# A windowed attention and a Fourier mixing on one core: the attention's pace by a table of units, one input's searches over more projections, weight splits a projection earlier

## The chip, the cores and the metric

The kernel runs on one core of a Trainium2 chip. The metric is the device time of one execution in microseconds, and a kernel's time is the median of its runs. The engines are TensorE (PE; PEld is its weight load), VectorE (DVE), ScalarE (ACT), GpSimd (POOL) and SyncE (SP), which here issues most of the DMAs.

## What is computed

Two independent results stand side by side in the output. The first is attention over 2048 rows with 32 heads of 32 elements, in which each row sees the 256 rows up to itself. The second is the real part of a two-dimensional Fourier transform, written as products with given matrices.

```python
qkv = (x @ wqkv).reshape(B, S, 3, H, Dh)            # S 2048, D 1024, H 32, Dh 32
scores = einsum("bhqd,bhkd->bhqk", q, k) * Dh ** -0.5
mask = (i - j >= 0) & (i - j < 256)
p = softmax(where(mask, scores, -1e9))
a = (einsum("bhqk,bhkd->bhqd", p, v)) @ wo

u = einsum("bsd,ed->bse", xb, dft_hid_re)
w = einsum("bsd,ed->bse", xb, dft_hid_im)
b = einsum("ts,bse->bte", dft_seq_re, u) - einsum("ts,bse->bte", dft_seq_im, w)
out = concatenate([a, b], axis=-1)
```

Inputs and outputs are float32. The first input and its weights are drawn eight times larger than usual.

## The kernel before

**Numbers.** Every operand of a large product is split into two float16 parts: ACT writes the scaled high part and DVE the rest (`split`). A product is then three matmuls (`PASSES`). A split needs a scale, and the scale needs the operand's largest magnitude: DVE searches each piece (`top`), a transpose on PE spreads the result (`scale_of`; its tile is called `pt_...`), and DVE makes the scale.

**Projections.** The list `order` holds 96 of them, n = 0 to 95: q, k and v for eight groups of four heads. Each is 24 matmuls of 512 columns into one of three PSUM banks; ACT and DVE empty the bank (`yq`, `yk`, `yv`) and SP stores it to DRAM (`qk`, `vs`). What else must happen meanwhile is entered in `tasks` with `at(n, ...)`, and is issued ahead of projection n. A weight that projection n uses first is loaded at n - 6 (`w_load`), searched at n - 4 (`w_top`), and scaled and split at n - 2 (`w_finish`). `scan("B", 16, 22, 1)` loads the 16 pieces of the second input at n = 22 to 37 and searches each one projection later; its scale follows at n = 40. From n = 41 on (`xp`) that scale is used to split the same input.

**Units.** The Fourier part follows as four rounds of twelve units, (p, c) = (0,0), (0,1), (1,0), (1,1). In a round, x0 to x3 are the hidden transform of four pairs of row blocks and c0 to c7 the sequence transform of eight pairs. A unit is seven products of twelve matmuls (`seven`), 84 in all. The work for unit n + 1 is done during unit n: for a c unit DVE and ACT search and split the two loaded pieces (`u_top`, `u_step`); for an x unit SP only loads finished pieces (`x_left`, tiles `un_a`, `un_c`, `un_b` and a part of `reg`). So DVE has little of this kind to do in c7 and x0. In x3 and c0 it also turns the x units' results into operands (`t_last`, line 795). In round (0,0) the c units store their results plainly through SP; later rounds add them to what stands in DRAM by accumulating stores that POOL issues (`store`, line 1069). The eight units `po` of the output projection end the program.

**Attention.** It is a generator, `attention()`, of 256 blocks: a block is one tile of 128 rows for two heads. A block goes through these steps: PE writes scores (`s`, `far`; three buffers), DVE masks (L237) and finds the row maximum (L239), ACT makes the bias (L242) and the exponentials (L249), ACT and DVE split them into `hl` (L252, L253; three buffers), SP transposes `hl` into `t` by DMA (L255), POOL masks two corners (`z_step`, L267 and L269), and PE multiplies with v (`pv`) six blocks later (`LAG`). Every fourth block, `o_step` divides by the row sum, splits, transposes through SP (`ot`) and stores (`ots`).

**Pace.** `tick(n)` is called after every few matmuls of projections and units. It adds `n * rate[0]` to a counter and advances the generator by half a block for each whole number. So the generator's instructions stand between those of the projections and units, and PE, which works in program order, waits there if a block's input is late. Before, `rate[0]` is `base * 0.6` in projections and `base` in units, with 0.2 of it in x3. By the formula `base` is 0.1217, so a projection takes 24 x 0.1217 x 0.6 / 2 = 0.88 blocks and a unit 84 x 0.1217 / 2 = 5.1, x3 1.0. A block may start only when its k and v are stored (`ready`).

The order of instructions on DVE, ACT, POOL and SP is laid down by a scheduler when the program is built; the programmer's order is its starting point.

Of the kernel before, what the change touches and what calls it, by code (L numbers as in the profile page):

```python
# [25 lines left out]
NG = H // HG  # L26
# [3 lines left out]
NCH = S // CH  # L30
QB = CH // P
# [7 lines left out]
LAG = 6  # L39
# [14 lines left out]
def fused_kernel(ctx: ExitStack, tc: tile.TileContext, xa, wqk, wv, wo, xb, wd, cs, out):  # L54
# [44 lines left out]
    def bank(name):  # L99
        nbank[0] += 1  # L100
        return ps_m.tile([P, CH], F32, tag=f"m{nbank[0] % 3}", name=name)
# [260 lines left out]
    def product(ps, lhs, rhs, n=ND):  # L362

        m = 0
        for d in range(n):
            for hl, hr in PASSES:
# [6 lines left out]
    order = ([("q", g, c) for c in range(NCH) for g in range(4)] + [("k", 0, c) for c in range(NCH)]  # L373
             + [("v", 0, t) for t in range(NT)]
             + [("k", g, c) for g in (1, 2, 3) for c in range(NCH)]
             + [("v", 1, t) for t in range(NT)]
             + [(kd, g, c) for g in range(4, NG) for kd in "qk" for c in range(NCH)])
    tasks = {}

    def at(n, f, *args):  # L380
        tasks.setdefault(n, []).append((f, args))


    START = 24
    LAST = 4
    SHARE = {"p": 0.6, "x": (1.0, 1.0, 1.0, 0.2), "c": 1.0}
    base = 2.0 * (NG * NCH * 2 * QB + 2 * LAG) / (
        24 * (len(order) - START) * SHARE["p"] + 84 * (4 * sum(SHARE["x"]) + (24 + LAST - 0.7) * SHARE["c"]))
    rate = [base * SHARE["p"]]

    wraw, wun, vw, xraw, held = {}, {}, {}, {}, {}
    scw = const.tile([P, 2, NG, 2], F32, name="scw")
# [128 lines left out]
        use.setdefault((kd, g), n)  # L521
    for (kd, g), n in use.items():
        if kd in "qk" and n >= 4:
            at(n - 6, w_load, kd, g)
            at(n - 4, w_top, kd, g)
            at(n - 2, w_finish, kd, g)
    for g in range(NG):
        at(max(use["q", g], use["k", g], 11), scores_scale, g)

# [20 lines left out]
    at(20, wv_known)  # L550
    def scan(key, k, n, step):
        for i in range(k):
            at(n + step * i, scan_load, key, i)
            at(n + step * i + 1, scan_top, key, i, k)
        at(n + step * (k - 1) + 3, scan_scale, key)

    scan("wd1", 8, 9, 1)
    scan("B", 16, 22, 1)
    scan("wd0", 8, 40, 4)
    scan("wo", 8, 73, 2)  # L560
    at(72, fa_known)
# [278 lines left out]
    with tc.tile_pool(name="pa", bufs=2) as pa:  # L840
        def qk_out(kd, g, c, ps, f):
            y = pa.tile([P, 2, CH], F16, tag="yq", name=f"y{kd}{g}_{c}")
            behind_act[:] = [nc.scalar.activation(y[:, 0], ps, AF.Copy, scale=f)]
            behind[:] = [vec(nc.vector.scalar_tensor_tensor, y[:, 1], ps, f, y[:, 0],
                             op0=ALU.mult, op1=ALU.subtract)]
            a = "qk".index(kd)
            for j, part in enumerate(((0, 1, 0), (0, 0, 1))[a]):
                nc.sync.dma_start(qk[g, c, j, :, :, a].rearrange("d h t -> (d h) t"), y[:, part])

        def d_out(g):  # L850
            qk_out("q", g, 0, direct.pop(g), f0[:, g:g + 1])

        w_top("q", 0)
        x_top(0, (0, 1, 2, 3))
        d_mm(0, range(0, 4))
        w_scale("q", 0)
        d_mm(0, range(4, 8))
        w_top("q", 1)
        d_mm(1, range(0, 1))
        x_scale(0)  # L860
        d_known(0)
        d_mm(1, range(1, 3))
        w_scale("q", 1)
        d_known(1)
        d_out(0)
        w_split("q", 0)
        w_top("q", 2)
        d_mm(1, range(3, 8))
        x_top(1, (0, 1))
        d_out(1)  # L870
        d_mm(2, range(0, 2))
        w_scale("q", 2)
        d_known(2)
        x_top(1, (2, 3))
        d_mm(2, range(2, 8))
        w_top("q", 3)
        d_mm(3, range(0, 2))
        x_scale(1)
        x_split(1, (0, 1))
        d_out(2)  # L880
        d_mm(3, range(2, 4))
        w_scale("q", 3)
        d_known(3)
        x_split(1, (2,))
        d_mm(3, range(4, 8))
        x_split(1, (3,))
        w_split("q", 1)
        d_out(3)

        for n, (kd, g, c) in enumerate(order):  # L890
            if n < 4:
                continue
            if n == 22:
                first_cm.__exit__(None, None, None)
                wx_pool = ctx.enter_context(tc.tile_pool(name="wx", bufs=1, side="right"))
                cellx["wx"] = wx_pool.tile([P, 3 * 2 * 4 * CH], F16, name="wx")
                att_cm = tc.tile_pool(name="att", bufs=2, side="right")
                cell["att"] = att_cm.__enter__()
                agen[0] = attention()
                upcoming[0] = next(agen[0])  # L900
            for f, args in tasks.pop(n, ()):
                f(*args)
            ps = bank(f"p{kd}{g}_{c}")
            if kd == "v":
                t = c
                product(ps, lambda h, d: xin[:, t // 4, h, d, t % 4 * P:t % 4 * P + P],
                        lambda h, d: reg2[:, g, h, d])
                y = pa.tile([P, H // 2, VW], F16, tag="yv", name=f"yv{g}_{t}")
                nc.gpsimd.memset(y[:, :, DH:DH + 1], 1.0)
                nc.gpsimd.memset(y[:, :, 2 * DH + 1:], 0.0)  # L910
                f = vf[:, g, t // 4:t // 4 + 1]
                pv = ps.rearrange("p (h d) -> p h d", d=DH)
                behind_act[:] = [nc.scalar.activation(y[:, :, :DH], pv, AF.Copy, scale=f)]
                behind[:] = [nc.vector.scalar_tensor_tensor(y[:, :, DH + 1:2 * DH + 1], pv, f, y[:, :, :DH],
                                                            op0=ALU.mult, op1=ALU.subtract)]
                nc.sync.dma_start(vs[t, :, g * (H // 2) * VW:(g + 1) * (H // 2) * VW],
                                  y.rearrange("p h w -> p (h w)"))
            else:
                u = wun[kd, g]
                product(ps, lambda h, d: u[:, h, d], lambda h, d: xin[:, c, h, d])  # L920
                qk_out(kd, g, c, ps, DOWN if kd == "q" else kf[:, c:c + 1])
            if kd == "v" and g == 0 and c % 4 == 3:
                ready.add((0, c // 4))
            if kd == "v" and g == 1 and c == NT - 1:
                pass
            if kd == "k" and g > 0:
                ready.add((g, c))
# [101 lines left out]
    with tc.tile_pool(name="pb", bufs=1) as pb:  # L1029
# [15 lines left out]
        for r in range(4):  # L1045
            x0, c0 = 12 * r, 12 * r + 4
            for j in range(4):
                n = x0 + j
# [5 lines left out]
            for j in range(8):  # L1054
                n = c0 + j
# [18 lines left out]

        x_left(0, "t")
        for n, (kind, p, c, i) in enumerate(units):
            rate[0] = base * (SHARE["x"][i] if kind == "x" else SHARE["c"])
            if kind == "x":
                y1, y2 = ytile(), ytile()

                def x_hook(pos):
                    (t_last if i > 1 else t_now)(i, pos, y2, y1)
                    hook(n, pos)

                if i < 2:
                    for turn in range(4):
                        do(n + 1, turn, t_then, i, turn, y2, y1)
                seven(f"p1_{n}", i, uns.pop(n), slot, y1, y2, 4.0 * DOWN, lambda t, y: None, x_hook)
                continue
            if p == 1 and c == 1:  # L1090
                if i == LAST:

                    while agen[0] is not None:
                        if next(agen[0], 0) == 0:
                            agen[0] = None
                    att_cm.__exit__(None, None, None)
                    late.append(ctx.enter_context(tc.tile_pool(name="late", bufs=8, side="right")))
                    raw = [[load_raw(wo[b % 2, 2 * (b // 2) + k], [2, CH], f"wo{b}_{k}", late[0]) for b in range(4)]
                           for k in range(2)]
                    for k in range(2):  # L1100
                        for j, f in enumerate(wo_blocks(raw[k], k)):
                            turn = 2 + (7 * k + j) * 3 // 2
                            do(n + turn // 7, turn % 7, f)
                    do(n + 2, 3, o_load, 0)
                    do(n + 2, 5, o_load, 1)
                    do(n + 3, 2, o_blocks, late, 0)
            y1, y2 = ytile(), ytile()
            f = fu.pop(n)

            def out_y(t, y):  # L1110
                dst, src = out[t * P:t * P + P, D:], y.rearrange("p e c -> p (e c)")
                if p == 0 and c == 0:
                    nc.sync.dma_start(dst, src)
                else:
                    do(n + 1, t % 2 == 0, store, dst, src)

            seven(f"p2_{n}", i, uns.pop(n), lambda pos: tsum[:, TPOS[pos]], y1, y2, f, out_y,
                  lambda turn: hook(n, turn))
# [61 lines left out]
```

## Time and profile before

| | us |
|---|---|
| median of three runs (1760.23 to 1774.22) | 1770.59 |
| the profiled execution | 1775.21 |
| its span | 1773.5 |
| DVE busy | 1381.1 (78%) |
| ACT busy | 1116.0 (63%) |
| POOL busy | 431.5 (24%) |

The first projection of the list that the loop runs starts about 35 us into the span, the units at 561.1 us and `po` at 1623.5 us. The shares above are means over stages that differ, so the prediction reads windows: a window row gives a stretch of time, its length, each engine's busy time in it with the number of instructions, the clock that TensorE was granted (1.00 is full), the mean busy share of the DMA engines and GB/s. A busy PE is modelled, since matmuls are pipelined. In a timeline row stand the start, the duration, the engine and line, and in brackets how long the engine sat idle before and what released it; SPq is the time that SP's queue takes to issue a DMA, not the transfer.

### The profile page before, as it was taken

The numbers are of one execution on the slowest core, as the hardware profiler recorded it, in microseconds if no ns is written. First come the engines' busy times: TensorE is split into PE (matmuls) and PEld (weight loads), VectorE is DVE, ScalarE is ACT, GpSimd is POOL, SyncE is SP. The second block draws the span as 40 slices with busy tenths as digits, with TensorE's granted clock in tenths as the row PEclk, the third lists the DMA queues.
The fourth block names the chain that finished last, engine by engine and source line by source line (L and its number), as shares of the span: only waits on it lengthen the run. The fifth ranks groups of instructions, "written<-read, shape, count | busy, mean of one in ns | idle before, by whom it ended". The sixth has DMA issues, their size and how long they took to land.

```text
span 1773.5 us, 30898 instructions
## 1 busy us (share of the span) xinstructions
PE 1710.9 (96%) x10980; PEld 854.1 (48%) x10980; DVE 1381.1 (78%) x2365; ACT 1116.0 (63%) x1939; POOL 431.5 (24%) x698
## 2 busy tenths in 40 slices
PE   9999999999999999999999989999898998999998
PEld 4444454545545545555544544545444444444443
DVE  7878987888894899985998866899686697586542
ACT  3335565665564888886878866888685686463322
POOL 0000221322132223332333423325243323100000
PEclk9999999999999999999999999999999999999999
DMA  9649999999999849999999999959989966854431
GB/s 344 199 158 281 323 283 300 286 270 310 270 253 259 198 100 210 213 209 237 194 282 172 207 163 229 206 115 186 186 171 204 205 144 105 231 99 95 131 95 72
DMA packets 473084, 363.32 MB, mean 205 GB/s; under 512 B 377440, under 2 KB 410208, under 8 KB 471648
## 3 DMA queue, kind: packets, MB, share of 16 engines
q1 hardware_dynamic: 466016, 336.17, 76.2%
q0 software_dynamic: 6912, 25.17, 8.9%
q8 instruction: 86, 1.41, 0.3%
q14 instruction: 70, 0.57, 0.1%
HBM read 178.52 MB, written 109.31 MB: 162 GB/s over the span
## 4 chain that ended last, share of the span: by engine, by line
PE 59%; DVE 18%; DMA 12%; ACT 5%; issue 4%; SPq 1%; POOL 1%; DVEq 0%; ACTq 0%; POOLq 0%
PE p_a L113 15%; PE pv L113 9%; PE p_b L113 7%; DMA t<-hl 7%; PE pq L113 7%; PE pk L113 6%; PE po_a L113 5%; PE p_c L113 4%; PE po_b L113 2%; PE s L113 2%; DVE hl L253 2%; DVE mx L239 2%; DVE reg L795 2%; DVE raw_u L752 1%; DVE y L996 1%
## 5 line engine op out<-in xcount | busy, mean ns | idle before, releaser
L249 ACT ACTIVATE s<-s,bias,escs 128x256 f32<-128x256 f32 (+1 forms) x512 | 270.1, 528 | 11.7
L253 DVE TENSOR_TENSOR hl<-s,hl 128x512 f16<-128x512 f32 (+1 forms) x256 | 170.6, 667 | 92.6 <-ACT hl L252 91.8
L113 PE MATMUL p_a<-reg,un_c 128*128 128x512 f16 x960 | 229.5, 381 | 7.7 <-ACT y L994 7.6
L267 POOL TENSOR_SCALAR_AFFINE_SELECT z<-t 128x512 f16<-128x512 f16 x224 | 171.9, 770 | 248.6 <-PE pv L113 128.2
L242 ACT ACTIVATE bias<-mx,pshift,escs 128x2 f32<-128x2 f32 x256 | 98.3, 384 | 168.2 <-DVE mx L239 165.7
L113 PEld LDWEIGHTS <-reg 128*128 128x128 f16 x1344 | 129.4, 98 | 143.0 <-issue 3.0
L246 POOL TENSOR_SCALAR mark<-bias 128x1 f32<-128x1 f32 x128 | 50.9, 398 | 570.3 <-ACT bias L242 547.3
L252 ACT ACTIVATE hl<-s 128x512 f16<-128x512 f32 (+1 forms) x256 | 148.8, 581 | 55.2 <-DMA t<-hl 49.8
L269 POOL TENSOR_SCALAR_AFFINE_SELECT t<-t 128x512 f16<-128x512 f16 x224 | 174.3, 783 | 12.4
L113 PE MATMUL pk<-reg,wu_k 128*128 128x512 f16 x768 | 174.6, 381 | 2.7 <-DVE wu_k L120 2.7
L113 PEld LDWEIGHTS <-un_b 128*128 128x128 f16 x1152 | 110.0, 98 | 132.7 <-issue 12.6
L239 DVE TENSOR_REDUCE mx<-s 128x2 f32<-128x512 f32 (+1 forms) x256 | 171.0, 668 | 2.9
L113 PE MATMUL pv<-reg,reg 128*128 128x512 f16 x768 | 171.9, 379 | 0.0
L113 PEld LDWEIGHTS <-un_c 128*128 128x128 f16 x1152 | 110.0, 98 | 127.3 <-issue 12.3
L113 PEld LDWEIGHTS <-un_a 128*128 128x128 f16 x1152 | 110.2, 98 | 121.5 <-issue 7.1
L113 PE MATMUL pq<-reg,wu_q 128*128 128x512 f16 x672 | 150.0, 379 | 3.8 <-DVE yq L120 2.9
L113 PE MATMUL p_b<-reg,un_b 128*128 128x512 f16 x576 | 139.7, 382 | 11.9 <-DVE reg L795 4.9
L113 PE MATMUL p_a<-reg,un_a 128*128 128x512 f16 x576 | 138.4, 382 | 3.4 <-DVE y L996 3.4
L113 PE MATMUL p_c<-reg,un_a 128*128 128x512 f16 x576 | 136.5, 379 | 0.0
L113 PEld LDWEIGHTS <-qk 96*128 96x128 f16 x1056 | 88.3, 98 | 79.8 <-issue 10.6
L237 DVE COPY_PREDICATED s<-upper,far 128x256 f32<-128x256 uint32 x224 | 94.4, 421 | 35.7 <-PE s L113 35.4
L113 PEld LDWEIGHTS <-wu_k 128*128 128x128 f16 x768 | 74.5, 98 | 85.4 <-DVE wu_k L120 3.2
(196 smaller groups left out, 3076.4 us busy)
## 6 DMA issues: line engine op xcount, KB each, us to landing
raw_u<-in_cs_dram SPq DMA_DIRECT2D x64, 512.0 KB, 4.9
qk<-qk SPq DMA_DIRECT2D x64, 384.0 KB, 5.3
out_dram<-y POOLq DMA_DIRECT2D x36, 512.0 KB, 8.0
qk<-yq SPq DMA_DIRECT2D x96, 128.0 KB, 4.2
qk<-yk SPq DMA_DIRECT2D x96, 128.0 KB, 3.7
xs<-wx SPq DMA_DIRECT2D x24, 512.0 KB, 5.0
wds<-wx SPq DMA_DIRECT2D x20, 512.0 KB, 5.7
vs<-yv SPq DMA_DIRECT2D x32, 264.0 KB, 4.4
```

The source lines that it names most:

```text
L113: fixed[:] = [nc.tensor.matmul(*args, **kwargs)]
L237: nc.vector.copy_predicated(s[:, :, P:], upper2, d["far"] if nb == 3 else never2)
L239: nc.vector.tensor_reduce(mx, sv, axis=AX.X, op=ALU.max, negate=True)
L242: nc.scalar.activation(bias, mx, AF.Identity, bias=pshift, scale=es)
L246: marks[:] = [nc.gpsimd.tensor_scalar(mark, bias[:, 0:1], 1.0, None, op0=ALU.mult)]
L249: nc.scalar.activation(sv[:, h], sv[:, h], AF.Exp, bias=bias[:, h:h + 1], scale=es)
L252: nc.scalar.activation(hi, sv, AF.Copy)
L253: behind[:] = [nc.vector.tensor_tensor(lo, sv, hi, op=ALU.subtract)]
L267: nc.gpsimd.affine_select(out=z, in_=pk, compare_op=ALU.is_gt, fill=0.0, base=0, pattern=[[0, 4], [-1, P]], channel_multiplier=1)
L269: nc.gpsimd.affine_select(out=pk, in_=pk, compare_op=ALU.is_ge, fill=0.0, base=0, pattern=[[0, 4], [1, P]], channel_multiplier=-1)
L752: nc.vector.tensor_tensor(o, a, b, op=op)
L795: nc.vector.tensor_tensor(lo, src, hi, op=ALU.subtract)
```

## The change

```diff
     START = 24
     LAST = 4
-    SHARE = {"p": 0.6, "x": (1.0, 1.0, 1.0, 0.2), "c": 1.0}
-    base = 2.0 * (NG * NCH * 2 * QB + 2 * LAG) / (
-        24 * (len(order) - START) * SHARE["p"] + 84 * (4 * sum(SHARE["x"]) + (24 + LAST - 0.7) * SHARE["c"]))
-    rate = [base * SHARE["p"]]
+    FIRST = (7.5, 5.2, 4.8, 0.4)
+    SECOND = (1.8, 4.4, 4.4, 4.4, 4.4, 4.4, 4.4, 7.5)
+    EARLY = {n: (0.85, 1.1, 1.05, 0.9, 1.0, 1.1)[(n - START) // 12] for n in range(START, len(order))}
+    in_units = 4 * sum(FIRST) + 3 * sum(SECOND) + sum(SECOND[:LAST]) - 0.7 * SECOND[LAST - 1]
+    early = (NG * NCH * 2 * QB + LAG - in_units) / sum(EARLY.values())
+    rate = [0.0]
...
-            at(n - 6, w_load, kd, g)
-            at(n - 4, w_top, kd, g)
-            at(n - 2, w_finish, kd, g)
+            at(n - 7, w_load, kd, g)
+            at(n - 5, w_top, kd, g)
+            at(n - 3, w_finish, kd, g)
...
     def scan(key, k, n, step):
         for i in range(k):
-            at(n + step * i, scan_load, key, i)
-            at(n + step * i + 1, scan_top, key, i, k)
-        at(n + step * (k - 1) + 3, scan_scale, key)
+            at(n + int(step * i), scan_load, key, i)
+            at(n + int(step * i) + 1, scan_top, key, i, k)
+        at(n + int(step * (k - 1)) + 3, scan_scale, key)
...
-    scan("B", 16, 22, 1)
+    scan("B", 16, 17, 1.4)
...
+            rate[0] = 2 * early * EARLY.get(n, 0.85) / 24
             ps = bank(f"p{kd}{g}_{c}")
...
-            rate[0] = base * (SHARE["x"][i] if kind == "x" else SHARE["c"])
+            rate[0] = 2 * (FIRST if kind == "x" else SECOND)[i] / 84
```

`FIRST` and `SECOND` give the blocks of each x and c unit directly: 7.5 in x0 and in c7, 0.4 in x3, 1.8 in c0, 4.4 in c1 to c6. `in_units` comes to 190.6 blocks, so `early` is (262 - 190.6) / 72 = 0.99, and `EARLY` scales it for six stretches of twelve projections: 0.84, 1.09, 1.04, 0.89, 0.99, 1.09 blocks a projection. In the built program the score matmuls of 72 blocks now stand in projections, against 64; x0 and c7 hold 7 or 8, against 5 or 6; c0 holds 2, against 4 to 6; c1 to c6 of the first three rounds hold 26, 26 and 27, against 30, 30 and 31. In round (1,1) the last block's scores move from c0 to c1. The number of instructions of each kind stays as it was.

The searches of the second input now start five projections earlier, 16 of them over 22 projections, and end one projection later, at n = 39; the scale falls at n = 41, the projection in which it is first used. All steps of a q or k weight move one projection ahead.

**DVE, ahead of the second group of k weights.** The rows run from the emptying of one v projection's bank (`yv`) to the split of the first weight of group 1 (`wu_k`), which projection 36 uses; `yv_14` is the bank of projection 34. Before:

```order
L914 SCALAR_TENSOR_TENSOR yv_14_1815<-pv_14_1773,vf,yv_14_1815 128x16x32
L120 RECIPROCAL scw<-scw 128x1
L120 TENSOR_REDUCE top_B<-raw_B_1767 128x1
L477 TENSOR_SCALAR e_1_1913<-scw,sc_X 128x1
L239 TENSOR_REDUCE mx_1804<-s_1798 128x2
L120 SCALAR_TENSOR_TENSOR wx<-wx,vwd 128x1024
L253 TENSOR_TENSOR hl_1744<-s_1730,hl_1744 128x512
L301 TENSOR_REDUCE o_0_1_1846<-pv_1845 128x132
L120 SCALAR_TENSOR_TENSOR wu_k_1761<-raw_wk_1461,scw,wu_k_1761 128x1024
```

After the change the same stretch, from `yv_13` on, reads:

```order
L917 SCALAR_TENSOR_TENSOR yv_13_1744<-pv_13_1679,vf,yv_13_1744 128x16x32
L120 TENSOR_REDUCE top_B<-raw_B_1673 128x1
L120 SCALAR_TENSOR_TENSOR wx<-wx,vwd 128x1024
L237 COPY_PREDICATED s_1764<-upper,far 128x2x128
L120 SCALAR_TENSOR_TENSOR wu_k_1667<-raw_wk_1411,scw,wu_k_1667 128x1024
L316 TENSOR_TENSOR ohl_0_0_1725<-o_0_0_1540,ohl_0_0_1725 128x256
L754 TENSOR_TENSOR wx<-wx 128x1024
L239 TENSOR_REDUCE mx_1770<-s_1764 128x2
L917 SCALAR_TENSOR_TENSOR yv_14_1799<-pv_14_1755,vf,yv_14_1799 128x16x32
```

The split has moved from eight rows behind `yv_14` to four ahead of it.

**SP, in c7 of round (0,0).** The rows run from the first to the second piece of the next x0's operand (`un_a`, `un_c`). `t` is a block's transpose, `ot` and `ots` the transpose and store of four finished blocks, `vt` and `qk` a load of v and of q and k. Before:

```order
L747 DMA un_a<-xs 128x2048
L255 DMA_TRANSPOSE t_9343<-hl_9340 128x8x128
L1113 DMA out_dram<-y_6136 128x1024
L255 DMA_TRANSPOSE t_9417<-hl_9414 128x8x128
L211 DMA vt_1_2_9544<-vs 128x4x132
L205 DMA qk_1_2_9542<-qk 96x2048
L255 DMA_TRANSPOSE t_9458<-hl_9455 128x8x128
L318 DMA_TRANSPOSE ot_0_3_9504<-ohl_0_3_9501 128x4x128
L337 DMA ots<-ot_0_3_9504 128x512
L255 DMA_TRANSPOSE t_9531<-hl_9528 128x8x128
L747 DMA un_c<-xs 128x2048
```

After:

```order
L749 DMA un_a<-xs 128x2048
L337 DMA ots<-ot_0_3_9445 128x512
L255 DMA_TRANSPOSE t_9480<-hl_9477 128x8x128
L255 DMA_TRANSPOSE t_9528<-hl_9525 128x8x128
L255 DMA_TRANSPOSE t_9576<-hl_9573 128x8x128
L205 DMA qk_1_3_9691<-qk 96x2048
L255 DMA_TRANSPOSE t_9612<-hl_9609 128x8x128
L318 DMA_TRANSPOSE ot_1_0_9655<-ohl_1_0_9652 128x4x128
L749 DMA un_c<-xs 128x2048
```

In both programs `ots` stands one to four rows behind the `ot` that it waits for, and transposes of later blocks stand behind it. In this stretch three block transposes now follow each other with nothing between them.

## The prediction, made before the changed kernel ran

> **What bounds the kernel now.** The page first, then the windows cut at each unit's first matmul, then the waits. Two lines of the page, busy time by engine and the chain that ended last:
>
> ```profile
> PE 1710.9 (96%) x10980; PEld 854.1 (48%) x10980; DVE 1381.1 (78%) x2365; ACT 1116.0 (63%) x1939; POOL 431.5 (24%) x698
> PE 59%; DVE 18%; DMA 12%; ACT 5%; issue 4%; SPq 1%; POOL 1%; DVEq 0%; ACTq 0%; POOLq 0%
> ```
>
> PE leads, but only 59% of the chain is PE; the rest is what PE waits for. The matmuls are the same after the change and their number too, so only waits can come or go. The windows show where they are:
>
> ```profile
> core 0: us, PE busy (x) PEld busy (x) DVE busy (x) ACT busy (x) POOL busy (x), PEclk, DMA share, GB/s
> 208.20:217.90 9.70, 7.01 (x27) 2.68 (x25) 9.04 (x12) 3.52 (x6) 0.24 (x2) 0.82 0.95 247
> 518.00:526.40 8.40, 5.88 (x32) 2.91 (x31) 8.30 (x21) 6.19 (x11) 2.69 (x3) 1.00 1.03 302
> 644.60:668.20 23.60, 21.97 (x180) 11.77 (x179) 23.60 (x45) 19.31 (x36) 8.14 (x8) 1.00 0.37 100
> 668.20:796.30 128.10, 128.10 (x970) 68.03 (x968) 118.00 (x228) 111.02 (x206) 48.15 (x71) 1.00 0.93 211
> 796.30:839.40 43.10, 42.97 (x323) 22.47 (x322) 24.37 (x49) 27.66 (x54) 11.04 (x21) 1.00 0.99 231
> 902.10:925.70 23.60, 21.53 (x155) 11.22 (x155) 23.23 (x44) 18.60 (x35) 9.14 (x10) 1.00 0.89 267
> 925.70:1072.60 146.90, 134.05 (x995) 69.73 (x994) 119.86 (x228) 110.94 (x207) 54.57 (x84) 0.97 1.07 184
> 1037.00:1072.60 35.60, 26.15 (x183) 13.06 (x181) 23.02 (x42) 19.95 (x36) 13.02 (x21) 0.86 0.97 191
> 1072.60:1117.10 44.50, 42.75 (x320) 22.39 (x319) 24.90 (x49) 27.25 (x55) 15.22 (x26) 1.00 1.15 237
> 1178.90:1202.40 23.50, 21.89 (x168) 11.53 (x168) 23.50 (x45) 19.18 (x35) 7.18 (x8) 1.00 0.62 142
> 1202.40:1345.60 143.20, 131.86 (x988) 69.13 (x986) 119.41 (x225) 109.06 (x202) 54.42 (x79) 0.98 1.00 182
> 1345.60:1395.80 50.20, 44.81 (x318) 23.27 (x318) 27.38 (x52) 29.34 (x58) 18.92 (x32) 0.93 1.08 208
> 1395.80:1421.90 26.10, 23.61 (x178) 12.03 (x177) 18.81 (x35) 16.46 (x31) 5.79 (x8) 0.93 0.91 198
> 1484.10:1511.80 27.70, 21.35 (x135) 10.31 (x134) 13.53 (x27) 10.37 (x16) 7.74 (x10) 0.88 0.94 129
> 1641.70:1659.80 18.10, 18.10 (x86) 8.16 (x85) 8.87 (x11) 5.24 (x7) 0.00 (x0) 1.00 0.41 117
> ```
>
> The last row is one `po` unit: 84 matmuls with nothing between them take 18.1 us. The six units c1 to c6 of round (0,0) (668.2 to 796.3) take 128.1 us with PE busy throughout; they hold 30 blocks, so a block adds (128.1 - 6 x 18.1) / 30 = 0.65 us to PE. A unit without waits is thus 18.1 us plus 0.65 a block.
>
> Now compare c1 to c6 of three rounds: 128.1, 146.9 and 143.2 us. VectorE's work in them is the same, 118.0, 119.9 and 119.4 us. So a VectorE at 92% makes no wait by itself. What rounds (0,1) and (1,0) have in addition are POOL's accumulating stores. Timeline rows of POOL, SP and PE, and two rows of the table of waits (total us, times, longest):
>
> ```profile
> 1022.40 1.82 POOL L1069 DMA_DIRECT2D out_dram<-y  x2 [0.26 <-DVE fu L732]
> 1029.10 8.36 SPq L255 DMA_TRANSPOSE t<-hl  x1
> 1504.80 0.24 PE L113 MATMUL pv<-vt,z 128*128 128x66 f16 x1 [5.94 <-POOL z L267]
> ACT hl L252 <- DMA t<-hl: 49.8, 17, 8.2
> POOL z L267 <- DMA t<-hl: 120.3, 38, 11.3
> ```
>
> Behind the pair of stores at 1022.4 a block's transpose keeps SP for 8.4 us; ACT and POOL then wait for transposes, and with three `hl` and three score buffers PE stops some blocks later (35.6 us for the unit at 1037.0). There is a second limit, VectorE itself, where it is full: the c0 windows at 644.6, 902.1 and 1178.9 have 98 to 100% of it.
>
> **The change part by part.**
>
> *Weights a projection sooner, searches spread.* Projection 36 takes 9.7 us, of which 24 matmuls need 24/84 x 18.1 = 5.2. The rest is this wait and the lower clock behind it (0.82):
>
> ```profile
> 211.47 6.78 PE L113 MATMUL pk<-reg,wu_k 128*128 128x512 f16 x23 [2.69 <-DVE wu_k L120]
> L120 DVE TENSOR_REDUCE top_B<-raw_B 128x1 f32<-128x1024 f32 x16 | 19.3, 1209 | 0.0
> ```
>
> The split now stands twelve rows further ahead, and in projections 24 to 35 VectorE has 8 searches of 1.21 us in place of 12. Taken: -4.5. The Trainium skill, TensorE: Matmul & The Clock Gate, section "Why this matters for your kernels", asks for no idle gap over about 3 us; here a wait of 2.69 us already lowered the clock, so the measurement decides, and short waits count at more than their length.
>
> The scale of the second input falls in the projection that first uses it (n = 41). ACT's first `xp` split then waits for one transpose and five short DVE instructions, and behind it on ACT stand exponentials and the emptying of a bank; PE has two other banks, 2 x 5.2 us of matmuls, as cover. Taken: 0, at most +2. A weight's load moves past one search load in SP's queue and keeps its buffer for four projections as before: 0.
>
> *More blocks in late projections.* A block costs VectorE L237, L239, L253 and half of L301:
>
> ```profile
> L239 DVE TENSOR_REDUCE mx<-s 128x2 f32<-128x512 f32 (+1 forms) x256 | 171.0, 668 | 2.9
> L253 DVE TENSOR_TENSOR hl<-s,hl 128x512 f16<-128x512 f32 (+1 forms) x256 | 170.6, 667 | 92.6 <-ACT hl L252 91.8
> L237 DVE COPY_PREDICATED s<-upper,far 128x256 f32<-128x256 uint32 x224 | 94.4, 421 | 35.7 <-PE s L113 35.4
> L301 DVE TENSOR_REDUCE o<-pv 128x132 f32<-128x264 f32 x128 | 54.4, 425 | 23.4 <-PE pv L113 23.0
> ```
>
> That is 2.0 us. In projections 84 to 90 the pace rises from 0.88 to 1.09: 7 x 0.21 x 2.0 = 2.9 us more, on a VectorE that is full at 518.0 (8.30 of 8.40). But that window's wait, 8.4 less 5.2 and 0.4 for a block's scores = 2.8 us, comes of two `pt` banks in one projection, and they now stand in two. Between +2.9 and -2.8 I take 0.
>
> *c0 with 2 blocks.* The three windows sum to 70.7 us; without waits 3 x (18.1 + 5.3 x 0.65) = 64.6. Three blocks fewer free 6 us of VectorE in each, and x3 has half a block less. Taken: -5 of 6.1.
>
> *c1 to c6 at 4.4.* Over the floor, rounds (0,1) and (1,0) lose 146.9 - 128.1 = 18.8 and, with 31 blocks, 143.2 - 128.8 = 14.4: 33.2. The stores stay, with the same bytes. What grows is reserve: six buffered blocks were 6 x 21.4 / 5.1 = 25 us and become 6 x 21.0 / 4.4 = 29 us, 4 us more for each late transpose, against overruns such as the 14.2 us at 1037.0. Between 0 and -33 I take half, -17.
>
> *The end.* The unit at 1484.1 takes 27.7 us; 84 matmuls and the v products of its last six blocks need about 18.1 + 2.0. Its 5.94 us wait is for blocks crowded into c0. At 1.8 and 4.4 a unit they come with a unit's time between scores and v. Taken: -7.
>
> *c7 and x0 at 7.5.* Here the change costs. Six such units (796.3, 1072.6, 1345.6) take 137.8 us now; without waits 6 x 18.1 + 31 x 0.65 = 128.8, so they already lose 9. VectorE has room (24.4 of 43.1). SP has not:
>
> ```profile
> 818.02 3.47 SPq L255 DMA_TRANSPOSE t<-hl  x1
> 821.58 0.53 SPq L747 DMA_DIRECT2D un_a<-xs  x1
> 822.20 0.38 SPq L1113 DMA_DIRECT2D out_dram<-reg  x1
> 823.14 1.62 SPq L318 DMA_TRANSPOSE ot<-ohl  x1
> 824.87 1.78 SPq L255 DMA_TRANSPOSE t<-hl  x1
> 830.50 0.34 SPq L337 DMA_DIRECT2D ots<-ot  x1
> 830.93 2.01 SPq L255 DMA_TRANSPOSE t<-hl  x1
> 833.67 1.23 SPq L255 DMA_TRANSPOSE t<-hl  x1
> 835.62 1.23 SPq L255 DMA_TRANSPOSE t<-hl  x1
> 838.83 1.30 SPq L255 DMA_TRANSPOSE t<-hl  x1
> ```
>
> A transpose keeps SP 1.84 us in the mean of these six, and from 826.65 to 830.50 SP stands at `ots` for 3.85 us. At 7.5 blocks: 7.5 x 1.84 + 1.9 x (1.62 + 3.85 + 0.34) + ten small DMAs at 0.43 = 29.1 us, against PE's 18.1 + 7.5 x 0.65 = 23.0. With 1.23 a transpose and no wait it is 17. So each unit loses between 0 and 6.1; I take 3, since at five blocks part of SP's waiting was free. Six units: +18, less the 9 lost now: +9. The first x0, at 561.1, has no stores beside it: 0.
>
> The sum against the profile's own time: 1775.2 - 4.5 - 5 - 17 - 7 + 9 = 1750.7. That execution lies 4.6 us above the median shown; what scatters is waits, and some two thirds of them stay, so 3 off: **1748**.
>
> **The rivals.**
>
> *SP's queue decides (slower).* In c7 and x0 SP's full 6.1 us a unit becomes PE waits. For: the rows above, and 7 or 8 blocks give SP no pause. Against: at 796.3 PE waits for almost nothing. Price: 36.6 us of waits; at 1037.0 a clock of 0.86 means 10 us at half speed, so 5 of the 14.2 us lost, a factor of 1.5: 55. The next x1 gets its operand late, as at 1395.8 (26.1 against 21.4), in three more rounds: +14. Less 9, and with the other terms: 1775.2 - 33.5 + 60 = 1801.7, or 1799. It decides the sign once c7 and x0 lose over (33.5 + 9) / 6 = 7.1 us each, clock and late loads included.
>
> *The stores decide, not the pace.* Transposes come late because of bytes in flight beside them; fewer blocks in c1 to c6 change nothing, nor does the end. For: equal VectorE work in 128.1 and 146.9 us. Against: reserve does grow. 1775.2 - 4.5 - 5 + 9 = 1774.7, or 1772. The Trainium skill, DMA: Bandwidth & Descriptors, section "Queues, rings and completion order", has each DMA engine take turns between queues packet by packet, whatever the issuing engine's pace; the row at 1029.10 agrees with that.
>
> *All waits go.* Reserve suffices in c1 to c6 and SP keeps up: 1775.2 - 4.5 - 2.8 - 6.1 - 33.2 - 7.6 - 9 = 1712, or 1711. For: PE without waits at 668.2. Against: DMA shares of 1.07 to 1.15 in the later rounds.
>
> **How the numbers follow.** About 1% (17.7 us, so 1753 and 1788) is what a measurement of this kernel can tell from no change. The forecast, 1735 to 1768, gets 0.40: 0.25 below 1753, 0.15 within. SP's queue 0.24: 0.19 slower, 0.05 within. The stores 0.18: 0.14 within, 0.03 slower, 0.01 faster. All waits gone 0.18, faster. Together faster 0.44, same 0.34, slower 0.22. The range 1718 to 1792 leaves out the lower half of the last case and the upper half of SP's, 0.2 in all.
>
> **What would show it.** Right: projection 36 at 5 to 6 us, c0 at 20 us, c1 to c6 of rounds (0,1) and (1,0) near 133 us each (floor 126), the last blocks without a long wait for z; c7 and x0 at 23 to 29 us. Wrong: c7 and x0 above 30 us with waits for transposes; c1 to c6 unchanged; new waits for banks in projections 36 to 47 or 84 to 91.

## The result, and the profile after

| | before | after |
|---|---|---|
| median, us | 1769.96 (1756.15 to 1783.33, 20 runs) | 1754.30 (1748.99 to 1762.63, 20 runs) |
| profiled execution, us | 1775.21 | 1749.20 |
| its span, us | 1773.5 | 1747.5 |

The ratio of the two kernels is 0.9924, with a 95% interval of 0.9905 to 0.9943. The change takes some 0.8% off. Here and below a median is of all runs, while a ratio leaves out the few that the chip ran in a slower state. The profiled executions lie further apart than the medians, 26.0 us against 15.7: the one before is 5.2 us above its median, the one after 5.1 us below.

Busy time by engine and the chain that ended last, from the page of the changed kernel:

```profile
PE 1704.0 (98%) x10980; PEld 852.0 (49%) x10980; DVE 1382.4 (79%) x2365; ACT 1113.5 (64%) x1939; POOL 422.4 (24%) x698
PE 65%; DVE 14%; DMA 11%; ACT 5%; issue 4%; SPq 1%; DVEq 0%; ACTq 0%; POOL 0%; POOLq 0%
```

PE holds 65% of the chain in place of 59%, with the same 10980 matmuls; VectorE's part, for which PE waits, fell from 18% to 14%. The windows of the changed kernel follow, cut at the same places as in the prediction (same columns): projection 36, projections 40 and 41, the first x0, c0 of round (0,0), c1 to c6 and then c7 with the next x0, and so on through the rounds, at the end x1 and c1 of round (1,1).

```profile
211.00:216.60 5.60, 5.60 (x35) 2.77 (x31) 5.60 (x8) 2.50 (x4) 2.96 (x6) 1.00 0.73 167
234.40:255.00 20.60, 14.94 (x84) 6.84 (x83) 12.66 (x31) 9.14 (x17) 4.57 (x7) 0.83 1.09 295
...
573.20:601.90 28.70, 25.17 (x218) 14.14 (x217) 17.75 (x37) 18.23 (x38) 10.98 (x20) 0.94 1.00 210
662.50:682.90 20.40, 19.79 (x119) 9.67 (x118) 17.52 (x31) 15.54 (x26) 3.57 (x5) 1.00 0.42 104
682.90:808.50 125.60, 125.60 (x917) 65.65 (x915) 107.51 (x207) 99.55 (x182) 32.90 (x54) 1.00 0.80 189
808.50:856.30 47.80, 46.47 (x412) 25.79 (x411) 33.22 (x65) 35.26 (x73) 19.77 (x36) 1.00 1.07 254
919.90:940.30 20.40, 19.45 (x115) 9.29 (x114) 18.58 (x37) 14.17 (x23) 2.14 (x2) 1.00 0.77 259
940.30:1066.10 125.80, 125.80 (x909) 65.72 (x908) 108.16 (x201) 101.49 (x184) 48.79 (x69) 1.00 1.03 188
1066.10:1121.70 55.60, 47.97 (x411) 25.51 (x410) 33.51 (x68) 35.04 (x73) 20.14 (x36) 1.00 1.04 211
1183.80:1202.90 19.10, 19.10 (x105) 9.15 (x104) 18.97 (x31) 15.24 (x26) 5.50 (x5) 1.00 0.32 94
1202.90:1329.10 126.20, 126.20 (x922) 66.19 (x921) 109.36 (x206) 101.55 (x184) 50.71 (x73) 1.00 1.02 196
1329.10:1382.50 53.40, 47.80 (x390) 26.00 (x388) 34.56 (x69) 35.29 (x73) 20.61 (x35) 0.94 1.09 211
1382.50:1404.20 21.70, 21.70 (x178) 11.66 (x179) 18.70 (x34) 16.90 (x34) 7.01 (x11) 1.00 1.01 214
1463.30:1484.40 21.10, 21.10 (x171) 11.10 (x169) 17.42 (x33) 15.74 (x28) 11.05 (x15) 1.00 0.76 147
```

Look first at c1 to c6 (682.9, 940.3 and 1202.9): PE is busy for the whole of all three windows, where two of them had lost 33 us. Then at c7 with x0: 47.8, 55.6 and 53.4 us, each with 15 blocks, against 2 x 18.1 + 15 x 0.65 = 46.0 without waits; these lose 1.8, 9.6 and 7.4. The first x0 takes 28.7 us and needs 18.1 + 8 x 0.65 = 23.3. In x0 of round (1,1), which starts at 1351.9, this is what PE and SP do:

```profile
1366.61 0.29 PE L113 MATMUL far<-qk,qk 96*128 96x128 f16 x1 [4.29 <-DMA qk<-qk]
...
1356.38 0.58 SPq L205 DMA_DIRECT2D qk<-qk  x1
1357.07 1.23 SPq L318 DMA_TRANSPOSE ot<-ohl  x1
1358.40 6.75 SPq L255 DMA_TRANSPOSE t<-hl  x1
1370.48 0.33 SPq L337 DMA_DIRECT2D ots<-ot  x1
```

PE waits for a load of q and k that was issued 10 us earlier. A block's transpose keeps SP for 6.75 us, and then SP stands at `ots` until 1370.48, for 5.33 us.

A wait that was not there before stands in projections 40 and 41, 20.6 us for two projections. Timeline rows of PE and ACT there:

```profile
240.07 0.27 PE L166 MATMUL pt_wk<-ident,top_wk 128*128 128x128 f32 x1
240.19 0.27 PE L166 MATMUL pt_B<-ident,top_B 128*128 128x128 f32 x1
246.12 6.40 PE L113 MATMUL pk<-reg,wu_k 128*128 128x512 f16 x16 [5.66 <-DVE yk L120]
...
244.60 0.69 ACT L845 ACTIVATE yk<-pk,kf 128x512 f16<-128x512 f32 x1 [2.23 <-DMA qk<-yk]
```

PE waits 5.66 us for a bank that VectorE empties once ACT has; ACT had waited for `yk`'s buffer. Just ahead, two scale transposes (`pt_wk` and `pt_B`) take two of the three banks. The window's clock is 0.83.

### The profile page after: what moved, and what is told of

It reads as the page before. It is cut to its first block, busy times and chain, and to the rows that moved or that the text cites. A ratio compares the mean times of both kernels' runs of the same rounds, so it can differ in the third digit from the quotient of the medians.

```text
span 1747.5 us, 30939 instructions
## 1 busy us (share of the span) xinstructions
PE 1704.0 (98%) x10980; PEld 852.0 (49%) x10980; DVE 1382.4 (79%) x2365; ACT 1113.5 (64%) x1939; POOL 422.4 (24%) x698
## 4 chain that ended last, share of the span: by engine, by line
PE 65%; DVE 14%; DMA 11%; ACT 5%; issue 4%; SPq 1%; DVEq 0%; ACTq 0%; POOL 0%; POOLq 0%
PE p_a L113 18%; PE pv L113 11%; PE p_b L113 9%; PE pk L113 7%; PE p_c L113 5%; PE po_a L113 5%; DMA t<-hl 4%; PE pq L113 4%; PE po_b L113 2%; PE s L113 2%; DMA qk<-qk 2%; DVE hl L253 1%; DMA qk<-yq 1%; DVE reg L797 1%; ACT s L249 1%
## 5 line engine op out<-in xcount | busy, mean ns | idle before, releaser
L267 POOL TENSOR_SCALAR_AFFINE_SELECT z<-t 128x512 f16<-128x512 f16 x224 | 163.7, 736 | 241.0 <-PE pv L113 157.5
L246 POOL TENSOR_SCALAR mark<-bias 128x1 f32<-128x1 f32 x128 | 46.8, 366 | 569.4 <-ACT bias L242 544.4
L269 POOL TENSOR_SCALAR_AFFINE_SELECT t<-t 128x512 f16<-128x512 f16 x224 | 178.3, 801 | 12.4
L237 DVE COPY_PREDICATED s<-upper,far 128x256 f32<-128x256 uint32 x224 | 94.1, 420 | 28.7 <-PE s L113 28.2
```

The source lines that it names most:

```text
L237: nc.vector.copy_predicated(s[:, :, P:], upper2, d["far"] if nb == 3 else never2)
L246: marks[:] = [nc.gpsimd.tensor_scalar(mark, bias[:, 0:1], 1.0, None, op0=ALU.mult)]
L267: nc.gpsimd.affine_select(out=z, in_=pk, compare_op=ALU.is_gt, fill=0.0, base=0, pattern=[[0, 4], [-1, P]], channel_multiplier=1)
L269: nc.gpsimd.affine_select(out=pk, in_=pk, compare_op=ALU.is_ge, fill=0.0, base=0, pattern=[[0, 4], [1, P]], channel_multiplier=-1)
```

## The experiments

Each kernel ran beside the kernel before on the same chip. Below, "loses" means time above 18.1 us a unit (5.2 a projection) and 0.65 us a block, from each run's profile.

**Which part of the change does what.** The pace alone (the searches and weights as before):

```diff
-            at(n - 7, w_load, kd, g)
-            at(n - 5, w_top, kd, g)
-            at(n - 3, w_finish, kd, g)
+            at(n - 6, w_load, kd, g)
+            at(n - 4, w_top, kd, g)
+            at(n - 2, w_finish, kd, g)
...
-    scan("B", 16, 17, 1.4)
+    scan("B", 16, 22, 1)
```

> The pace by kind of unit alone, with the searches and the weights' splits where they stood before. By the terms as the two traces measured them: c0 -5, c1 to c6 about -33, the end -7.6, c7 and x0 +15, so about -30 against before; the 9.7 us of projection 36 come back in place of the clash of two pt tiles in projection 40, so the time stands near 1750 us, within 5 us of the changed kernel. Rival, the clash comes from the pace (more blocks in projections 36 to 47): then projection 41 still waits over 4 us here and the time is near 1757 us.

Measured 1760.91 us, ratio 0.9950 (0.9921 to 0.9978), 11 us above the 1750 that was expected: faster than before, but perhaps by less than the whole change. And the rest alone (the kernel before with `n - 7, n - 5, n - 3` and `scan("B", 16, 17, 1.4)`):

> The searches spread and the weights a projection sooner alone, with the pace as before. Theory, two pt tiles that stand next to each other in projection 40 make PE wait at projection 41 whatever the pace: projection 36 gains 4.5 us, the wait at 518 us goes (-2.8) and 8.7 us are lost at projections 40 and 41; no change against before (1770 us, within 4). Rival, the clash needs the changed pace: 7 us faster than before, near 1763 us.

Measured 1779.57 us, ratio 1.0047 (1.0010 to 1.0084): a little slower, which neither expectation had. Projections 40 and 41 take 18.7 us in its profile, with the pace of before, so the neighbouring `pt` tiles make that wait whatever the pace. In the run of the pace alone they stand in projections 39 and 41, and PE's longest wait there is 2.05 us. The pace alone brings most of the gain, and the rest alone brings none.

**Is the wait at 40 and 41 worth its 8.9 us?** The changed kernel with the second input's tile in projection 39:

```diff
-    scan("B", 16, 17, 1.4)
+    scan("B", 16, 16, 1.4)
```

> The changed kernel with the searches of the second input one projection sooner, so that its pt tile stands in projection 39 and the weights' in 40. Theory, the neighbouring pt tiles cost the 8.7 us of projections 40 and 41: 8 us faster than the changed kernel, near 1746 us, and projection 41 takes 5.2 us without a wait. Rival, ACT is late there for another reason (the store of yk that keeps its buffer, the exponentials): the wait stays over 4 us and the time within 2 us of the changed kernel.

Measured 1754.90 us, ratio 0.9930 (0.9899 to 0.9960): no change. Windows of projections 36 to 47 and 48 to 51 in this run:

```profile
208.87:281.00 72.13, 70.58 (x481) 35.89 (x478) 60.57 (x112) 42.55 (x75) 18.18 (x33) 1.00 1.04 274
281.00:311.08 30.08, 25.28 (x164) 12.38 (x162) 22.87 (x35) 17.63 (x31) 6.87 (x14) 0.94 1.06 305
```

ACT's timeline there:

```profile
280.13 0.69 ACT L845 ACTIVATE yk<-pk,kf 128x512 f16<-128x512 f32 x1 [2.18 <-DMA qk<-yk]
283.43 1.15 ACT L126 ACTIVATE wx<-wx,vB 128x1024 f16<-128x1024 f32 x1 [2.60 <-DMA xs<-wx]
```

The same stretch in the changed kernel, projections 36 to 51:

```profile
210.95:313.11 102.16, 96.50 (x644) 48.45 (x641) 84.98 (x147) 61.26 (x106) 29.14 (x48) 0.97 1.03 283
```

Both take 102.2 us. The wait left projection 41, and one stands at 48 in its place, where ACT waits twice for buffers whose stores haven't landed (in the run of the pace alone, projections 48 to 51 take 28.1 us as well, against 23.4 in the changed kernel). So the first theory saw the cause of that wait rightly and its price wrongly.

**What makes c1 to c6 wait?** First the stores: the kernel before with plain stores in place of POOL's accumulating ones.

```diff
-                nc.gpsimd.dma_start(dst, src, accum_op=ALU.add)
+                nc.gpsimd.dma_start(dst, src)
```

> The kernel before, with POOL's accumulating stores made plain ones (the same bytes from SBUF, no addition to what stands in DRAM, which is left out). Theory, the accumulating stores hold back the transposes and so make the 33 us of waits in c1 to c6 of rounds (0,1) and (1,0): these windows fall to about 128 us each and the run is about 30 us shorter. Rival, the waits come from the pace (VectorE at 92% with no reserve for any late transfer): they stay above 20 us in the two rounds together.

Measured 1729.86 us (one run), 36.5 below the median before. Its windows of c1 to c6 in rounds (0,1) and (1,0):

```profile
927.70:1056.40 128.70, 128.70 (x995) 68.59 (x994) 118.25 (x224) 110.60 (x205) 52.58 (x83) 1.00 1.02 208
1184.40:1313.40 129.00, 128.89 (x987) 68.52 (x985) 117.95 (x225) 109.15 (x202) 51.43 (x79) 1.00 0.88 201
```

With the old pace and VectorE at 92% there is no wait without accumulation. So these waits need the accumulating stores. Then the pace: c1 to c7 at 5.1 again, with c0 kept light.

```diff
-    FIRST = (7.5, 5.2, 4.8, 0.4)
-    SECOND = (1.8, 4.4, 4.4, 4.4, 4.4, 4.4, 4.4, 7.5)
+    FIRST = (5.8, 5.2, 4.8, 0.4)
+    SECOND = (1.8, 5.1, 5.1, 5.1, 5.1, 5.1, 5.1, 5.1)
```

> The changed kernel with c1 to c7 at 5.1 blocks a unit again and x0 at 5.8; c0 keeps 1.8. Theory A, the slower pace in c1 to c6 is what gives reserve: the waits come back there, 20 us or more in rounds (0,1) and (1,0), x0 and c7 lose 15 us less, and the time is within 1% of the kernel before (1760 to 1770 us). Theory B, c0's lighter start was enough (the crowd of c0's blocks is what ran into the later units): c1 to c6 stay within 5 us of their floor and the run is faster than the changed kernel, 1740 us or less.

Measured 1765.15 us, ratio 0.9981 (0.9949 to 1.0012): what the change won is gone, as theory A had it. The place of the waits does not fit theory A: c1 to c6 lose only 4.2 and 2.3 us, within the 5 us of theory B, while c7 of round (0,1) loses 11.1 and x0 of round (1,1) 7.3. So a light c0 alone does not hold the gain. That the slow pace of c1 to c6 does is the likelier reading and is not fully shown, since this run changes c7 and x0 too.

**A third cause: `ots`.** SP's table of waits before (us in total, times, longest) begins with a row that the prediction did not use; after the change it still leads:

```profile
SPq L337 <- DMA ot<-ohl: 158.1, 55, 8.6
```

```profile
SPq L337 <- DMA ot<-ohl: 130.9, 54, 8.5
```

SP stands at every store `ots` until the transpose `ot` has landed, and block transposes queue behind it. The Trainium skill, DMA: Bandwidth & Descriptors, section "Two DMAs through the same engine are not ordered", says that only the completion semaphore orders two DMAs and that the issuing engine has to wait for it; the rows agree, and show how long SP stands for it in a queue that issues other work. Held in SP's order until three more blocks' transposes are issued:

```diff
-            nc.sync.dma_start_transpose(t[:, :4 * min(nb, 2)], hl[:, :4 * w])
+            last_t[:] = [nc.sync.dma_start_transpose(t[:, :4 * min(nb, 2)], hl[:, :4 * w])]
...
-                    nc.sync.dma_start(*store_o.pop(0))
+                    with tc.issue_after(last_t[0].ins):
+                        nc.sync.dma_start(*store_o.pop(0))
```

First in the changed kernel:

> The changed kernel with the store of an attention output (ots) held in SP's order until the transposes of three more blocks have been issued. Theory, SP standing 3 to 6 us at ots is what makes the transposes late in c7 and x0: those units' waits (about 24 us in seven units) fall by half or more, 10 us or more faster, near 1744 us. Rival, the transposes are late because the transfers themselves are slow there, and SP would only stand elsewhere: x0 of rounds (1,0) and (1,1) still lose 6 us or more each and the time changes by less than 3 us.

Measured 1747.10 us, ratio 0.9875 (0.9828 to 0.9922), between the two expectations. In its profile (1759.26 us, the slowest of its six executions) the first x0 takes 25.2 us in place of 28.7, but x0 of rounds (1,0) and (1,1) 31.3 and 35.6. SP's timeline in the last of these:

```profile
1359.50 1.22 SPq L318 DMA_TRANSPOSE ot<-ohl  x1
1360.82 11.12 SPq L255 DMA_TRANSPOSE t<-hl  x2
1372.03 0.54 SPq L211 DMA_DIRECT2D vt<-vs  x1
1372.67 7.01 SPq L255 DMA_TRANSPOSE t<-hl  x2
```

No `ots` stands there, and two transposes still keep SP for 11.1 us. The transfers themselves are slow there, as the rival had it: two `ot` land in 10.3 us in the median, against 3.8 in c1 to c6 of round (0,1) of the same execution. Then the same edit in the kernel before, and nothing else:

> The kernel before, with only the store of ots held in SP's order until the transposes of three more blocks have been issued; pace, searches and weights as before. Theory, SP standing at ots (for a transpose that an accumulating store holds back) is what makes one late transfer into a queue of late transposes: c1 to c6 of rounds (0,1) and (1,0) lose 15 us or less in place of 33, and the run is 10 to 25 us faster than before, 1745 to 1760 us. Rival, only the reserve that the slower pace gives helps: those waits stay over 25 us and the time is within 5 us of before.

Measured 1745.15 us, ratio 0.9879 (0.9838 to 0.9921). Windows of c1 to c6 in rounds (0,1) and (1,0):

```profile
928.50:1057.20 128.70, 128.70 (x994) 68.60 (x993) 118.45 (x224) 110.84 (x205) 56.30 (x83) 1.00 1.09 208
1191.50:1321.00 129.50, 129.00 (x987) 68.54 (x986) 118.77 (x225) 109.22 (x202) 58.09 (x79) 1.00 1.05 201
```

Its row of SP's waits, where 158.1 us stood:

```profile
SPq L338 <- DMA ot<-ohl: 15.2, 2, 10.7
```

Pace, c0 and searches are as before, the accumulating stores are in place, and c1 to c6 take what they take without accumulation. So the place of this one store decides these waits too, and moving it is worth about as much as the whole change (the intervals overlap). Not every wait is gone: c7 of the same two rounds loses 5.5 and 6.7 us.

That it is the length of SP's standing that counts is not shown. With plain stores SP stands at `ots` nearly as long as before (19.6 us against 21.9 in c1 to c6 of round (0,1)), and PE waits for nothing. And with `ots` held back another row appears, which was 0.4 us before:

```profile
SPq L318 <- DMA ots<-ot: 32.8, 24, 4.1
```

The next `ot` now waits until the held store has freed its buffer. The table of DMA issues for c1 to c6 of round (0,1) (count, KB each of a plain transfer, median us to landing) shows what else changed. Before:

```profile
out_dram<-y POOLq DMA_DIRECT2D x9, 512.0 KB, 9.9
...
t<-hl SPq DMA_TRANSPOSE x32, 6.0
ot<-ohl SPq DMA_TRANSPOSE x8, 5.5
```

With `ots` held back:

```profile
out_dram<-y POOLq DMA_DIRECT2D x9, 512.0 KB, 6.8
...
t<-hl SPq DMA_TRANSPOSE x31, 4.9
ot<-ohl SPq DMA_TRANSPOSE x8, 3.8
```

In round (1,0) the same stores land in 7.1 us before and 6.7 with `ots` held back, with 14.4 us lost in the one and 0.7 in the other, so their landing time by itself doesn't tell where PE waits.

**How much pace is too much.** x0 lighter and c1 to c6 at 4.8, without and with `ots` held back:

```diff
-    FIRST = (7.5, 5.2, 4.8, 0.4)
-    SECOND = (1.8, 4.4, 4.4, 4.4, 4.4, 4.4, 4.4, 7.5)
+    FIRST = (5.5, 5.2, 4.8, 0.4)
+    SECOND = (1.8, 4.8, 4.8, 4.8, 4.8, 4.8, 4.8, 7.5)
```

> The changed kernel with x0 at 5.5 blocks and c1 to c6 at 4.8 (c7 stays at 7.5). Theory, x0's waits are a matter of blocks beside its operand loads and stores: x0 of rounds (1,0) and (1,1) take 24 us or less in place of 31, the first x0 24 in place of 29, c1 to c6 stay within 4 us of their floor; 12 to 16 us faster than the changed kernel, near 1740 us. Rival, the delay is made in c7 and only shows in x0: x0 keeps 5 us or more of waits in rounds (1,0) and (1,1), and the time changes by less than 4 us.

> The run before this one (x0 at 5.5, c1 to c6 at 4.8) with the store of ots also held behind three more transposes in SP's order. If SP's standing at ots costs of itself, another 5 us or more off it; if the transfers are what is slow, the two are within 3 us of each other.

Measured 1771.26 us, ratio 1.0021 (0.9991 to 1.0051), a miss by 30 us, and 1744.86 us, ratio 0.9890 (0.9852 to 0.9927), well over 5 us off it. The windows of c1 to c7 in round (1,0), without and with:

```profile
1203.50:1377.70 174.20, 156.05 (x1142) 81.82 (x1140) 131.32 (x249) 123.89 (x229) 61.98 (x94) 0.95 1.05 177
```

```profile
1186.00:1337.70 151.70, 150.09 (x1141) 79.58 (x1139) 129.72 (x245) 123.12 (x228) 63.38 (x94) 1.00 1.06 204
```

At 4.8 blocks a unit most of the waits are back (22.5 us between the two windows) as long as SP stands at `ots`. The two profiles exaggerate: the first is of an execution of 1778.77 us, the second of 1733.49, the fastest of its six. The medians differ by 26.4 us all the same. Of the three paces tried with SP at `ots`, only 4.4 leaves c1 to c6 without waits; but pace alone doesn't rank the others, since in rounds (0,1) and (1,0) they lost 6.5 us in all at 5.1 and 23.2 at 4.8 with c7 at 7.5.

**What x0 still loses.** The changed kernel with plain stores:

> The changed kernel with POOL's accumulating stores made plain ones (the addition to what stands in DRAM is left out). Theory, the 19 us of waits in c7 and x0 come of transposes that accumulating stores hold back, as in c1 to c6 before: x0 of rounds (0,1), (1,0) and (1,1) take 23 to 25 us, and the run is about 15 us shorter. Rival, eight blocks in a unit are more than the queue of transposes carries whatever the stores do: x0 of rounds (1,0) and (1,1) stay over 28 us, like the first x0, which has no such store beside it.

Measured 1744.46 us (one run). x0 takes 28.7 (the first), 29.3 and 27.3 us (rounds (1,0) and (1,1)), against 28.7, 31.4 and 30.7 in the changed kernel: without accumulation 5.5 us less are lost in two units, and the rest stays. It lies between the theories, nearer to the rival.

**Combining.** From the run with x0 at 5.5 and `ots` held back, with `scan("B", 16, 16, 1.4)` and

```diff
-    EARLY = {n: (0.85, 1.1, 1.05, 0.9, 1.0, 1.1)[(n - START) // 12] for n in range(START, len(order))}
+    EARLY = {n: (0.95, 0.95, 0.95, 0.95, 1.05, 1.15)[(n - START) // 12] for n in range(START, len(order))}
```

> The run with x0 at 5.5, c1 to c6 at 4.8 and ots held back, and in addition the two pt tiles apart (the second input's searches a projection sooner) and fewer blocks in projections 36 to 59 (0.95 in place of 1.1 and 1.05; more in 24 to 35 and 84 to 95). Theory, projections 36 to 59 wait because blocks, the stores of yk and the splits of wx share transfers that are full there: both stretches together lose 3 us or less in place of 7.8, near 1739 us. Rival, the wait moves to where the blocks went (24 to 35, 84 to 95): the projections as a whole end no sooner than 571 us and the time is within 3 us of that run (1745 us).

Measured 1752.69 us, ratio 0.9912 (0.9884 to 0.9940): no faster than the run it came from, whose interval it overlaps, and a miss for both expectations. Projections 36 to 51 fell from 101.0 to 95.7 us, as the theory had it, but the projections ended only 0.9 us sooner (568.3 against 569.2): the rest was given back on the way. The units behind lost more, though the profile to compare with is that run's fastest execution. And a last version:

```diff
+    FIRST = (5.2, 5.2, 4.8, 0.4)
+    SECOND = (1.8, 4.9, 4.9, 4.9, 4.9, 4.9, 4.9, 6.8)
+    EARLY = {n: (0.95, 0.95, 0.95, 0.95, 1.05, 1.05)[(n - START) // 12] for n in range(START, len(order))}
...
+    scan("B", 16, 16, 1.4)
```

> A version put together from the runs so far: the changed kernel with ots held back, x0 at 5.2, c1 to c6 at 4.9, c7 at 6.8, the two pt tiles two instructions of VectorE further apart (projections 39 and 40) and 0.95 blocks a projection up to 71, 1.05 behind. If the waits add up as the earlier profiles have them (projections 36 to 59 about 3 us, the rest as with x0 at 5.5 and ots held back) it is near 1738 us. Rival, the waits left over scatter from run to run and move with every edit: 1742 to 1748 us, no different from the two kernels with ots held back.

Measured 1766.65 us, ratio 1.0008 (0.9972 to 1.0044): a miss for both. Its profiled execution, 1754.66 us, is the fastest of its runs; there PE waits 8.24 us in x0 of round (1,0) for q and k that SP issued late, behind an `ots` that took 6.74 us to issue and two transposes of 4.95 and 2.44 us. What its slower runs lose was not seen. This version holds `ots` back too, so that edit does not pay at every pace. No version is clearly better than the kernel before with `ots` held back (1745.15), the changed kernel with it (1747.10), or that with x0 at 5.5 as well (1744.86); their intervals overlap.

## Why the prediction was right, and by which steps

The time forecast was 1748 and 1754.3 came. That is faster, as forecast, but by 15.7 us and not by the 22.6 of the forecast, and it lies just inside the band above 1753 that the prediction called no change. By the profiled execution, 1750.7 was forecast and 1749.2 came, and that closeness is luck: terms off in opposite directions made it, and the two executions lie 5 us off their medians on opposite sides.

| term | predicted, us | measured, us |
|---|---|---|
| projection 36 | -4.5 | 5.6 - 9.7 = -4.1 |
| `pt` tiles, 36 to 47 and 84 to 91 | 0, at most +2 | +8.9 at 40 and 41, -2.8 at 518 |
| c0 | -5 | 6.1 - 1.7 lost: -4.4 |
| c1 to c6 | -17 | 33.2 - 0.3 lost: -32.9 |
| the end | -7 | 7.6 lost, now no wait: -7.6 |
| c7 and x0 | +9 | 18.8 - 9 lost: +9.8 |
| the first x0 | 0 | +5.4 |
| sum | -24.5 | -27.7 (spans: -26.0) |

One gain stands in no row: x1 of round (1,1), late for its operand before, went from 26.1 to 21.7 us. Small losses elsewhere, most of them in the projections, make up for it.

*Projection 36, c0, the end.* Right in place and size.

*c1 to c6.* The direction was right and the size half of what came; the term is the sum's largest error. The step that failed is the size: "Between 0 and -33 I take half, -17", where 32.9 went. The 4 us of reserve set against overruns of 14.2 gave no ground for any figure in between. What stands ahead of it, that VectorE at 92% makes no wait and that the accumulating stores do, is true, as the run with plain stores shows, but not the whole: where `ots` stands in SP's queue matters as much. The prediction saw SP standing there for 3.85 us and charged it to c7 and x0 only, though the row of SP's waits, 55 times and 158.1 us, covers the whole program. The runs support three conditions that must meet: accumulating stores, `ots` close behind its `ot`, and too little reserve. Plain stores, a later `ots` or the slower pace each end the waits in c1 to c6, and the change took the third. At that pace SP stands at `ots` about as long (20.6 us in c1 to c6 of round (0,1), 21.9 before), so the pace changes what a stand costs and not its length. How the three act together is not shown.

*The rival that the stores decide, not the pace* had its first half right. Its conclusion, that fewer blocks change nothing, fell: with 26 and 27 blocks 32.9 of the 33.2 us are gone. The row at 1029.10, which the rival takes as agreeing with turns by packet, shows only that SP was held for 8.36 us, not how the DMA engines share their time.

*c7 and x0.* The term came out as forecast by luck. "I take 3" for each unit is the mean of none in c7 (23.1, 24.2 and 22.8 us) and of 2.0, 8.8 and 7.4 in x0, two of them above the 6.1 taken as the most. At 31.4 and 30.7 us these two pass the 30 us that the prediction gave as a sign of being wrong. The causes have other shares too. It took SP's transposes at 1.84 us and the stand at `ots`; with `ots` held back, x0 of the late rounds lost as much, and with plain stores it lost 2 to 3 us a unit less and kept the rest. (Both together were not tried.) In the later rounds fewer blocks helped: at 5.5, x0 of the last three rounds takes 21.8, 26.7 and 24.5 us, and with `ots` held back as well 21.8, 21.8 and 27.1. The first x0, where "no stores beside it: 0" was wrong, has eight blocks too; with six it took 29.8 us and, with `ots` held back as well, 24.4, so its cause stays open. SP's queue did not decide the sign: 18.8 us in six units is 3.1 each, under the 7.1 at which it would have.

*The `pt` tiles.* A new wait for a bank in projections 36 to 47, another sign of being wrong that the prediction gave, came. "ACT's first `xp` split then waits" was the wrong instruction to look at. What cost 8.9 us was that two transposes, one moved by the weights' edit and one by the searches', met in projection 40 and held two of three banks, so the cover of two banks was gone. This stood in the order of instructions and could have been read there. But the search run shows that the price is not 8.9: taking the wait away at 41 brought nothing, since the stretch of projections 36 to 51 took 102.2 us both ways.

What stays open: why the searches and weights cost 0.5% beside the old pace and bring 0.3% or so beside the new one (0.9950 to 0.9924, whose intervals overlap), what the later place of `ots` changes if it is not the length of SP's standing, and why the last version is slow. The builder's scheduler lays every queue anew with each edit, and what else it moved was not compared. No run with the searches in their old place and `ots` held back at the new pace was made.

## What to carry to other kernels

A queue's own table of waits shows a store that waits for a transfer issued just before it; everything behind it waits too. Moving that one store back by a few rows was worth at least as much here (0.9879) as the new pace for the whole attention (0.9950), though not in every combination. A wait isn't always worth its length, since the next one may take its place: take it away alone and see where the time goes before adding it to a sum. And two edits that each move an instruction into the same place must be looked at together in the built order.

## What the runs showed of the hardware

A DMA share of 1.0 and more is no sign by itself that PE will wait: c1 to c6 of rounds (0,1) and (1,0) ran without a wait at 1.03 and 1.02 after the change and at 1.09 and 1.05 with `ots` held back, while the same units lost 33 us before at 1.07 and 1.00.

The accumulating stores keep the DMA engines busy about twice as long as plain ones of the same size. Rows of the queue that POOL's stores use (packets, MB, share of the 16 engines' time) for c1 to c6 of round (0,1), before and with plain stores:

```profile
q0 software_dynamic: 1728, 6.29, 28.8%
```

```profile
q0 software_dynamic: 1728, 6.29, 16.4%
```

These are 28.8% of 147 us and 16.4% of 129 us, 42 and 21 us of all 16 engines, for the same packets and bytes.

A wait of PE under 3 us can be followed by half clock, but is not always: before, after waits of 2.69 us (to 211.47) and 2.49 us (to 1401.95) the granted clock was 0.50 for over 3 us, and after one of 2.52 us (to 526.37) it stayed at 1.00.
